# An attention and routed-MLP kernel: another order of the first units, wider matmuls there, and a first batch whose rows are picked by a 0/1 product

## The chip, the cores and the metric

The kernel runs on one core of one Trainium2 chip. The metric is the device time in microseconds, the median of several runs. TensorE (PE) multiplies, VectorE (DVE) and ScalarE (ACT) work elementwise, GpSimd (POOL) does small elementwise work and issues the gathers and scatters, and SyncE (SP) issues nearly all other transfers. Each engine works through its own list in order; semaphores tie the lists together.

## The reference

The inputs q, k, v are 8 batches x 8 heads x 576 positions x 64, in float32. The first part is linear attention; the second routes 128 of the 576 rows of each batch through an MLP:

```python
q_s = softmax(q, axis=-1)                 # over the 64 columns
k_s = softmax(k, axis=2)                  # over the 576 positions
kv = einsum('bhsd,bhse->bhde', k_s, v)    # 64 x 64 for each head
x = einsum('bhsd,bhde->bhse', q_s, kv)    # then heads side by side: (8, 576, 512)

scores = einsum('bsd,d->bs', x, w_gate)
out = x.copy()
for b in range(8):
    top = argpartition(-scores[b], 128)[:128]
    y = maximum(x[b, top] @ w1, 0) @ w2   # 512 -> 1024 -> 512
    out[b, top] = x[b, top] + sigmoid(scores[b, top])[:, None] * y
```

## The kernel before

The work is cut into 16 units: unit u is half of the heads (four) of batch u // 2. The 576 positions of a head lie on 128 partitions in five blocks of 64 or 128 rows, and each step has two halves (`i`), one for each pair of heads.

For one unit the steps are: `load` brings k, v and q; `k_exp`, `q_exp` (ScalarE) take exponentials; `v_copy` puts v beside a column of ones; `kv_mm` multiplies exp(k) by v, 20 matmuls; `kv_out` takes the reciprocal of the sums (`krec`), copies the product to `kv_w` and adds a column, the product with the gate weights `wg`; `q_t` turns exp(q) with TensorE into PSUM, from where one operation for each half scales it by `krec` into `qT`; `x_mm` multiplies `qT` by `kv_w`; `x_out` scales the result by the reciprocals of q's sums into `xs` and writes the sums for the score; `x_store` sends `xs` to the output.

For one batch follow: `score` (adds the gate's sums), `score_row` (five TensorE transposes lay the scores along the free axis on every partition; ScalarE copies them to `srow`), five `compare`, each counting for 128 rows how many scores are larger (`rank`), and `pick`: it compares the rank with the slot numbers to a 0/1 tile `hit`, multiplies this by row numbers and scores on TensorE, and gathers the 128 rows from the output in memory (`xr`). `gate` makes the sigmoid, `turn` transposes the rows to `xT`, eight pieces `mlp1` (four 128x128x128 products each) and eight pieces `mlp2` (one 128x128x512 each) are the MLP, and `finish` adds `xr` to the gated result and scatters it.

The order is written out by hand; nothing is rearranged later. Units 0 to 3 run in a first loop (lines 520 to 566) with `fill`, matmuls on ones whose result nobody reads. Then stage s (lines 571 to 628) runs, for unit s, `q_t`, `x_mm`, `x_out`, `x_store`, for unit s + 1 `kv_mm` and `kv_out`, and between them the MLP of batch (s - 4) // 2: `mlp1` in even stages, `mlp2` in odd ones. A load tile serves every third unit (`LD = 3`). Every transfer takes one of eight semaphores in turn, so that it waits for the transfer eight places before it. PSUM banks rotate by two under each of the names `tp`, `x` and `mm`; a step that writes a bank waits until the bank's last contents are read. At the end a number tells whether all sums are in range; if not, `general` computes everything once more in another way. It isn't entered here.

Of the kernel before, what the change touches and what calls it, by code (L numbers as in the profile page):

```python
# [8 lines left out]
F32 = mybir.dt.float32  # L9
# [8 lines left out]
def kernel(  # L18
# [39 lines left out]
    WARM = 20  # L58
# [4 lines left out]
    n_sl = -(-capacity // P)  # L63
    cuts = [capacity * i // n_sl for i in range(n_sl + 1)]
# [18 lines left out]

    units = [(b, qd) for b in range(B) for qd in range(NQ)]
# [7 lines left out]
    def load(u, which, queue=nc.sync):  # L92
        b, qd = units[u]
        for what in which:
            src = {"q": q, "k": k, "v": v}[what]
            t = raw[what][u % LD]
            first = src[b, 4 * qd].offset
            for n, rows in ((1, N2), (0, R)):
                queue.dma_start(
                    out=t[n::2, :, :rows].rearrange("p h r d -> p h (r d)"),  # L100
                    in_=bass.AP(tensor=src.tensor, offset=first + n * R * D,
                                ap=[[9 * D, 64], [SD, 4], [1, rows * D]]))
# [5 lines left out]
    load(0, "k")  # L108
    load(0, "v", nc.scalar)
    load(0, "q")  # L110
    load(1, "kvq")
    load(2, "kvq")

# [7 lines left out]

    wg = const.tile([P, NQ, 2, D], F32, name="wg")
    for h in range(2):
        nc.scalar.dma_start(out=wg[part(h)].rearrange("p a i d -> p (a i) d"),
                            in_=bass.AP(tensor=moe_w_gate.tensor, offset=moe_w_gate.offset + h * D,
                                        ap=[[0, 64], [2 * D, 2 * NQ], [1, D]]))
    warm = const.tile([P, 1], F32, name="warm")
    nc.scalar.activation(out=warm, in_=ones_b[:, :1], func=AF.Exp)
    w1 = const.tile([P, KD, F], F32, name="w1")
    w2 = const.tile([P, KF, DM], F32, name="w2")  # L130

# [55 lines left out]
    for r in range(R):  # L187
        nc.vector.tensor_scalar(not_before[:, r], order_minus_p, float(r * P), TINY, op0=OP.is_ge, op1=OP.mult)
# [42 lines left out]
    def q_t(u, i):  # L231

        if i == 0:
            st["qT", u] = at.tile([P, 2, R, 2, D], F32, tag="qT", name="qT")
        qe = st["qe", u] if i == 0 else st.pop(("qe", u))
        t_ps = ps.tile([P, 2, 512], F32, tag="x", name="x", bufs=2)
        for r in range(R):
            for a in range(2):
                nc.tensor.transpose(out=t_ps[:, a, r * 64:(r + 1) * 64],  # L239
                                    in_=qe[part(a), i, r].rearrange("p h d -> p (h d)"),  # L240
                                    identity=ident[part(a), part(a)])
        nc.scalar.activation(out=st["qT", u][:, i].rearrange("p r a c -> p a r c"),  # L242
                             in_=t_ps[:, :, :R * 64].rearrange("p a (r c) -> p a r c", r=R),
                             func=AF.Copy, scale=krec[:, u, i:i + 1])

    def x_mm(u, i):
# [4 lines left out]
        for r in range(R):  # L251
            for h, c in QUARTERS:
                nc.tensor.matmul(out=x[part(c), h, r * C:(r + 1) * C], lhsT=qT[part(h), i, r, c],  # L253
                                 rhs=kv_w[u % 2][part(h), i], start=True, stop=True)
# [4 lines left out]
    def x_out(u, i):  # L259
        b, qd = units[u]  # L260
        if qd == 0 and i == 0:
            xs[b] = xp.tile([P, R, NQ, 2, 2, D], F32, tag="xs", name="xs")
            sr[b] = md.tile([P, NQ * 2, G], F32, tag="sr", name="sr")
        x = st.pop(("x", u, i))[:, :, :R * C].rearrange("p h (r c) -> p h r c", r=R)
        rec = qrec[:, u, i].rearrange("p (h r) -> p h r", h=2)
        nc.vector.reciprocal(out=rec, in_=x[:, :, :, D])  # L266
        nc.vector.tensor_mul(xs[b][:, :, qd, i].rearrange("p r h d -> p h r d"), x[:, :, :, :D],  # L267
                             rec.to_broadcast([P, 2, R, D]))
        nc.vector.tensor_mul(sr[b][:, 2 * qd + i].rearrange("p (h r) -> p h r", h=2), x[:, :, :, D + 1], rec)

    def x_store(u):
        b, qd = units[u]
        for n, rows in enumerate((R, N2)):
            nc.sync.dma_start(
                out=bass.AP(tensor=out.tensor, offset=out[b, n * R].offset + 4 * D * qd,
# [4 lines left out]
    def score(b, up=2):  # L280

        raw_s = s_all[:, b]
        nc.vector.reduce_sum(out=raw_s, in_=sr.pop(b).rearrange("p a (h r) -> p r a h", h=2),
                             axis=AX.XY)
        s = md.tile([P, R], F32, tag="s", name="s")
        nc.vector.tensor_mul(s, raw_s, valid_r[:, up])
        nc.vector.tensor_add(s, s, valid_r[:, 1])
# [3 lines left out]
        for c in range(2, NV):  # L291
            nc.gpsimd.tensor_copy(out=vals[:, b, :, c], in_=raw_s if c == 2 else left)
            if c < NV - 1:
                nc.gpsimd.tensor_sub(left, raw_s if c == 2 else left, vals[:, b, :, c])

    def score_row(b):
        s = st["s", b]
        srow = md.tile([P, RP], F32, tag="srow", name="srow")
        for r0, r1 in ((0, N2), (N2, R)):
            t_ps = bank("tp", 2)  # L300
            for r in range(r0, r1):
                nc.tensor.transpose(out=t_ps[:, (r - r0) * P:(r - r0 + 1) * P],
                                    in_=s[:, r:r + 1].to_broadcast([P, P]), identity=ident)
            if r0 == 0:
                nc.scalar.copy(out=srow[:, :N2 * P], in_=t_ps)
            else:
                nc.scalar.copy(out=srow[:, N2 * P:], in_=t_ps[:, :P:2])  # L307
# [21 lines left out]
    def pick(b):  # L329

        rank = st.pop(("rank", b))
        st.pop(("s", b)), st.pop(("srow", b))
        for n, (k0, m) in enumerate(slots):
            hit = md.tile([P, R, P], BF16, tag="hit", name="hit", bufs=1)
            nc.vector.tensor_tensor(out=hit[:, :, :m], in0=slot_no[:, None, k0:k0 + m].to_broadcast([P, R, m]),
                                    in1=rank.to_broadcast([P, R, m]), op=OP.is_equal)
            c_ps = bank("tp", 2)
            for r in range(R):
                nc.tensor.matmul(out=c_ps[:m, :NV], lhsT=hit[:, r, :m], rhs=vals[:, b, r],
                                 start=(r == 0), stop=(r == N2))  # L340
            no = sl.tile([P, 2], F32, tag="no", name="no")
            idx = sl.tile([P, 1], I32, tag="idx", name="idx")
            nc.vector.reduce_sum(out=no[:m, 0:1], in_=c_ps[:m, 0:2], axis=AX.X)
            nc.vector.tensor_scalar(idx[:m], no[:m, 0:1], float((b + 1) * S - 1), None, op0=OP.min)  # L344
            nc.vector.reduce_sum(out=no[:m, 1:2], in_=c_ps[:m, 2:NV], axis=AX.X)  # L345
            xr = sl.tile([P, DM], F32, tag="xr", name="xr")
            nc.gpsimd.indirect_dma_start(  # L347
                out=xr[:m], out_offset=None, in_=out_rows[:(b + 1) * S],
                in_offset=bass.IndirectOffsetOnAxis(ap=idx[:m, :1], axis=0))
            st["pick", b, n] = xr, no, idx  # L350

    def gate(b, n):
        m = slots[n][1]
        xr, no, idx = st["pick", b, n]
        g = sl.tile([P, 1], F32, tag="g", name="g")
# [3 lines left out]
        st["pick", b, n] = xr, g, idx  # L359


    def turn(b, n):
        m = slots[n][1]
        xr = st["pick", b, n][0]
        xT = sl.tile([P, KD, P], F32, tag="xT", name="xT")
        t_ps = bank("mm", 2)
        for d in range(KD):
            nc.tensor.transpose(out=t_ps[:, d * m:(d + 1) * m], in_=xr[:m, d * P:(d + 1) * P],  # L368
                                identity=ident[:m, :m])
        nc.scalar.copy(out=xT[:, :, :m], in_=t_ps[:, :KD * m].rearrange("p (d c) -> p d c", d=KD))  # L370
# [23 lines left out]

    def finish(b, n):
        m = slots[n][1]
        xr, g, idx = st.pop(("pick", b, n))
        y_ps = st.pop(("y", b, n))
        o = sl.tile([P, DM], F32, tag="o", name="o")
        nc.vector.scalar_tensor_tensor(o[:m], y_ps[:m], g[:m], xr[:m], op0=OP.mult, op1=OP.add)  # L400
        nc.gpsimd.indirect_dma_start(  # L401
            out=out_rows[:(b + 1) * S], out_offset=bass.IndirectOffsetOnAxis(ap=idx[:m, :1], axis=0),
            in_=o[:m], in_offset=None)
# [34 lines left out]
    def general():  # L438
        for b in range(B):
# [16 lines left out]
            score_row(b)  # L456
            for r in range(R):
                compare_exact(b, r)
            pick(b)
            each(gate, b)  # L460
# [9 lines left out]
    def sums_in_range():  # L470
# [5 lines left out]
        for n, (src, op, bound) in enumerate(((rq, OP.max, 1.0 / LOW), (rk, OP.max, 1.0 / LOW), (sc, OP.max, FAR),  # L476
# [3 lines left out]
                                    op0=OP.is_le if op == OP.max else OP.is_ge)  # L480
        g_ps = bank("tp", 2)
# [8 lines left out]
    LAG = 4  # L490

    def load_w1(n):
        nc.sync.dma_start(out=w1[:, n], in_=moe_w1[n * P:(n + 1) * P])

    def load_w2(n):
        half = KF // 2
        nc.sync.dma_start(out=w2[:, n * half:(n + 1) * half],
                          in_=moe_w2[n * half * P:(n + 1) * half * P].rearrange("(f p) d -> p f d", p=P))

    EARLY = 4  # L500

    def fill(n):

        junk_ps = bank("mm", 2)
        for _ in range(n):
            nc.tensor.matmul(out=junk_ps, lhsT=ones_b[:, :P], rhs=ones_b, start=True, stop=True)

# [6 lines left out]
    k_exp(0)  # L514
    v_copy(0)
    kv_and_exp(0)
    load(3, "kvq")


    for s in range(EARLY):  # L520
        q_t(s, 0)
        q_t(s, 1)
        k_exp(s + 1)
        v_copy(s + 1, nc.gpsimd)
        fill(2)
        x_mm(s, 0)
        x_mm(s, 1)
        fill(2)
        if s == 2:
            kv_mm(s + 1)  # L530
            q_exp(s + 1, 0)
            fill(3)
            pick(0)
            x_out(s, 0)
            kv_out(s + 1)
            x_out(s, 1)
            x_store(s)
            q_exp(s + 1, 1)
        else:
            x_out(s, 0)  # L540
            x_out(s, 1)
            x_store(s)
# [114 lines left out]
```

## Time and profile before

| | us |
|---|---|
| median of three runs | 218.88 (217.52 to 220.17) |
| the profiled execution | 217.89 |
| its span, first to last instruction | 216.0 |
| TensorE busy | 197.5 |
| VectorE busy | 116.2 |
| ScalarE busy | 88.6 |
| GpSimd busy | 34.4 |
| transfers | 46.81 MB, 217 GB/s over the span |

Row 1 of the page gives busy time of each engine, its share of the span and the number of its instructions. The slices cut the span into 40 pieces of 5.4 us; a digit is the busy share in tenths. A line of the timeline or of a group reads: start, length, engine, line of the kernel, operation, what is written and what is read, number; in brackets the idle time of the engine ahead of it and what ended it. `PE` is the matmul itself, `PEld` the load of its weights. A float32 matmul is two records. Matmuls overlap, so that their price is the difference of two starts. A line of a table of windows has the stretch, its length, busy time and number for PE, PEld, DVE, ACT and POOL, then TensorE's clock, the share of the DMA engines and GB/s. In the chain of work that ended last, a line has a start, a length, the engine and what it did.

### The profile page before, as it was taken

Reading aid. Unit: us, or ns where it says so; the run is one execution under the profiler, and the core shown is the slowest. Engines: PE = TensorE matmul, PEld = TensorE weight load, DVE = VectorE, ACT = ScalarE, POOL = GpSimd, SP = SyncE. Lnnn points to the kernel's source line nnn. Section 1 sums busy time; section 2 is a strip of 40 time slices with the busy share of each in tenths; the row PEclk is TensorE's granted clock in tenths of the full one; section 3 lists DMA queues with packets and bytes.
Section 4 is the critical chain, followed back from the end, with each engine's and each line's share of the span. In section 5 each row is a group of like instructions: output and inputs, shape, how many; then the busy total and the mean of one; then the engine's idle time right before and its main releaser. Section 6 shows DMA issues by size and latency. Waiting matters only on the chain. (4 is left out here: it accounts for less than half of the span.)

```text
span 216.0 us, 7090 instructions
## 1 busy us (share of the span) xinstructions
PE 197.5 (91%) x3040; PEld 147.2 (68%) x3040; DVE 116.2 (54%) x359; ACT 88.6 (41%) x146; POOL 34.4 (16%) x78
## 2 busy tenths in 40 slices
PE   5987595999999999999999999999999989999960
PEld 2464462799749975897679776996599548749620
DVE  6552595668726774477626872596358665501010
ACT  2386374763626471746265443536263311211100
POOL 6022402300112012200320023001120112101010
PEclk9999999999999999999999999999999999999996
DMA  5999999999999997958594949421313041101001
GB/s 179 299 356 358 375 398 369 362 392 377 377 384 381 375 344 249 314 157 283 171 320 154 313 133 303 161 82 49 113 52 109 7 156 52 49 3 52 5 5 52
DMA packets 39335, 46.81 MB, mean 217 GB/s; under 512 B 2944, under 2 KB 36736, under 8 KB 39296
## 3 DMA queue, kind: packets, MB, share of 16 engines
q1 hardware_dynamic: 36928, 41.36, 56.4%
q0 software_dynamic: 1280, 4.20, 5.7%
q10 hardware_dynamic: 1088, 0.72, 1.1%
q8 instruction: 26, 0.43, 0.8%
q14 instruction: 13, 0.11, 0.2%
HBM read 34.73 MB, written 11.53 MB: 214 GB/s over the span
## 5 line engine op out<-in xcount | busy, mean ns | idle before, releaser
L382 PE MATMUL mm<-xT,w 128*128 128x128 f32 x512 | 62.1, 278 | 0.0
L382 PEld LDWEIGHTS mm<-xT,w 128*128 128x128 f32 x512 | 58.8, 192 | 2.3 <-ACT xT L370 1.5
L392 PE MATMUL mm<-w,hT 128*128 128x512 f32 x128 | 59.9, 603 | 0.0
L315 DVE SCALAR_TENSOR_TENSOR junk<-srow,s,not_before 128x576 bf16<-128x576 f32 x40 | 32.8, 819 | 8.3 <-ACT srow L307 7.2
L392 PEld LDWEIGHTS mm<-w,hT 128*128 128x128 f32 x128 | 22.5, 190 | 21.2 <-issue 20.4
L267 DVE TENSOR_TENSOR xs<-x,qrec 128x640 f32<-128x640 f32 x32 | 26.4, 825 | 1.1
L242 ACT ACTIVATE qT<-x,krec 128x640 f32<-128x640 f32 x32 | 23.9, 792 | 6.2 <-PE x L239 6.1
L400 DVE SCALAR_TENSOR_TENSOR o<-mm,g,xr 128x512 f32<-128x512 f32 x8 | 6.0, 751 | 37.7 <-PE mm L392 37.7
L202 ACT ACTIVATE qe<-q 128x640 f32<-128x640 f32 x32 | 23.6, 739 | 3.0 <-DMA q<-in_q_dram 2.8
L215 PE MATMUL tp<-v_ones,ke 128*64 128x65 f32 x640 | 22.6, 224 | 2.3 <-issue 2.1
L215 PEld LDWEIGHTS tp<-v_ones,ke 128*64 128x64 f32 x640 | 20.3, 137 | 5.3 <-issue 3.0
L253 PE MATMUL x<-kv_w,qT 64*64 64x66 f32 x1280 | 22.4, 221 | 0.0
L347 POOL DMA_INDIRECT xr<-out_dram,idx x8 | 8.0, 996 | 88.8 <-DVE qrec L266 72.6
L253 PEld LDWEIGHTS x<-kv_w,qT 64*64 64x64 f32 x1280 | 20.2, 134 | 2.6 <-ACT qT L242 0.8
L195 ACT ACTIVATE ke<-k 128x1280 f32<-128x1280 f32 x16 | 20.3, 1270 | 2.8 <-DMA k<-in_k_dram 2.8
L385 ACT ACTIVATE hT<-mm 128x512 f32<-128x512 f32 x16 | 9.5, 596 | 28.7 <-PE mm L382 28.7
L239 PEld LDWEIGHTS x<-ident,qe 64*128 64x128 f32 x320 | 11.7, 139 | 11.6 <-issue 5.0
L239 PE MATMUL x<-ident,qe 64*128 64x64 f32 x320 | 14.5, 229 | 4.9 <-issue 1.4
L266 DVE RECIPROCAL qrec<-x 128x10 f32<-128x10 f32 x32 | 6.9, 215 | 20.7 <-PE x L253 20.7
L401 POOL DMA_INDIRECT out_dram<-o,idx x8 | 10.1, 1269 | 46.8 <-DVE o L400 46.8
L226 ACT COPY kv_w<-tp 128x130 f32<-128x130 f32 x16 | 4.3, 266 | 31.4 <-DVE krec L224 31.4
L370 ACT COPY xT<-mm 128x512 f32<-128x512 f32 x8 | 4.7, 585 | 26.9 <-PE mm L368 26.9
(81 smaller groups left out, 126.0 us busy)
## 6 DMA issues: line engine op xcount, KB each, us to landing
k<-in_k_dram SPq DMA_DIRECT2D x16, 320.0 KB, 7.0
q<-in_q_dram SPq DMA_DIRECT2D x16, 320.0 KB, 6.1
out_dram<-xs SPq DMA_DIRECT2D x16, 320.0 KB, 2.9
v<-in_v_dram SPq DMA_DIRECT2D x15, 320.0 KB, 7.9
k<-in_k_dram SPq DMA_DIRECT2D x16, 256.0 KB, 7.2
q<-in_q_dram SPq DMA_DIRECT2D x16, 256.0 KB, 6.4
out_dram<-xs SPq DMA_DIRECT2D x16, 256.0 KB, 3.2
v<-in_v_dram SPq DMA_DIRECT2D x15, 256.0 KB, 7.7
```

Source lines behind the costliest of these rows:

```text
L195: nc.scalar.activation(out=ke, in_=raw["k"][u % LD], func=AF.Exp)
L202: nc.scalar.activation(out=st["qe", u][:, i], in_=qr[:, i], func=AF.Exp)
L215: nc.tensor.matmul(out=kv[part(h), i], lhsT=ke[:, 2 * i + h, r], rhs=vo[:, 2 * i + h, r], start=(r == 0), stop=(r == N2))
L239: nc.tensor.transpose(out=t_ps[:, a, r * 64:(r + 1) * 64], in_=qe[part(a), i, r].rearrange("p h d -> p (h d)"), identity=ident[part(a), pa ...
L242: nc.scalar.activation(out=st["qT", u][:, i].rearrange("p r a c -> p a r c"), in_=t_ps[:, :, :R * 64].rearrange("p a (r c) -> p a r c", r= ...
L253: nc.tensor.matmul(out=x[part(c), h, r * C:(r + 1) * C], lhsT=qT[part(h), i, r, c], rhs=kv_w[u % 2][part(h), i], start=True, stop=True)
L267: nc.vector.tensor_mul(xs[b][:, :, qd, i].rearrange("p r h d -> p h r d"), x[:, :, :, :D], rec.to_broadcast([P, 2, R, D]))
L315: nc.vector.scalar_tensor_tensor(junk, st["srow", b], st["s", b][:, r:r + 1], not_before[:, r], op0=OP.subtract, op1=OP.is_ge, accum_out=s ...
L382: nc.tensor.matmul(out=h_ps[:, f % 4 * m:(f % 4 + 1) * m], lhsT=w1[:, d, f * P:(f + 1) * P], rhs=xT[:, d, :m], start=(d == 0), stop=(d == ...
L385: nc.scalar.activation(out=hT[:, f - 3:f + 1, :m], in_=h_ps[:, :4 * m].rearrange("p (f c) -> p f c", f=4), func=AF.Relu)
L392: nc.tensor.matmul(out=st["y", b, n][:m], lhsT=st["hT", b, n][:, f, :m], rhs=w2[:, f], start=(f == 0), stop=(f == KF - 1))
L401: nc.gpsimd.indirect_dma_start(out=out_rows[:(b + 1) * S], out_offset=bass.IndirectOffsetOnAxis(ap=idx[:m, :1], axis=0), in_=o[:m], in_off ...
```

## The change

- The batches are worked in another order: batch `b` of the program is batch `(b - 1) % 8` of the data (`place`), so that the first one stands last in the output.
- Units 0 to 2 use a wide form: `q_t` has five 128x128 transposes for each half, not ten of 64 partitions; `x_mm` has ten matmuls with 128 columns of weights, not twenty of 64x64. For two halves VectorE scales `qT` in ScalarE's place. The fills are gone, and `WARM` falls from 20 to 12.
- The gate weights come as one row of 512, and two matmuls with ones spread them over the partitions. Three of five masks `not_before` are made later.
- `x_out` is parted into `x_sums` (the score's sums) and `x_scale`, so that the score can be taken before the scaling. `score_row` reads the raw scores, and ScalarE multiplies by the constant while it copies. GpSimd makes the masked scores `s`.
- For batch 0, `select` multiplies the rows in `xs` by a 0/1 tile on TensorE after each `compare`, which gives `xT` without memory. Its stores come in stage 5, its gather in stage 16, its last addition (`finish_rows`, on GpSimd) and scatter in stage 17.
- The stages begin with unit 3 (`LAG = 3`). In stages 3, 5 and 7 (`OWN`) the unit's own `kv_mm` runs in the stage, and that of the next unit at its end.
- Loads: k of unit 0 on two queues, then v and q, units 1 and 2, all of w1 in two column halves, unit 3, half of w2, unit 4, the other half; then unit s + 2 in stages 3 to 5, unit 8 in stage 6, 9 and 10 in stage 7, 11 and 12 in stage 8.

```diff
-    WARM = 20
+    WARM = 12
+    def place(b):
+        return (b - 1) % B
...
-    def q_t(u, i):
+    def q_t(u, i, on_vector=False, wide=False):
...
+        if wide:
+            to = st["qT", u][:, i].rearrange("p r a c -> p (r a c)")
+            src = t_ps.rearrange("p a c -> p (a c)")[:, :R * P]
+            for r in range(R):
+                nc.tensor.transpose(out=src[:, r * P:(r + 1) * P], in_=qe[:, i, r].rearrange("p h d -> p (h d)"),
+                                    identity=ident)
...
+        if on_vector:
+            nc.vector.tensor_scalar(to, src, krec[:, u, i:i + 1], None, op0=OP.mult)
...
+    def select(b, n, r):
+        k0, m = slots[n]
+        if r == 0:
+            st["select", n] = bank("mm", 2), md.tile([P, R, P], F32, tag="hit_f", name="hit_f", bufs=1)
+        t_ps, hit = st["select", n]
+        nc.vector.tensor_tensor(out=hit[:, r, :m], in0=slot_no[:, k0:k0 + m],
+                                in1=st["rank", b][:, r:r + 1].to_broadcast([P, m]), op=OP.is_equal)
+        row = xs[b][:, r].rearrange("p a i h d -> p (a i h d)")
+        for d in range(KD):
+            nc.tensor.matmul(out=t_ps[:, d * m:(d + 1) * m], lhsT=row[:, d * P:(d + 1) * P], rhs=hit[:, r, :m],
+                             start=(r == 0 and d == 0), stop=(r == N2 and d == KD - 1), skip_group_check=True)
+        if r == N2:
+            turned(b, n, t_ps)
...
+    def finish_gated(b, n):
+        m = slots[n][1]
+        o = sl.tile([P, DM], F32, tag="o_gated", name="o_gated", bufs=n_sl)
+        nc.scalar.activation(out=o[:m], in_=st.pop(("y", b, n))[:m], func=AF.Copy, scale=st.pop(("g", b, n))[:m])
+        st["o", b, n] = o
+    def finish_rows(b, n):
+        m = slots[n][1]
+        o = st.pop(("o", b, n))
+        nc.gpsimd.tensor_add(o[:m], o[:m], st.pop(("xr", b, n))[:m])
+        put(b, n, o)
...
+    ready(0)
+    q_exp(0, 0)
+    kv_mm(0)
...
+    set_not_before(range(2))
+    nc.vector.tensor_copy(out=wg.rearrange("p a i d -> p (a i d)"), in_=g_ps[:, :4 * D])
+    kv_out(0)
+    q_exp(0, 1)
...
+    q_t(0, 0, wide=True)
+    q_t(0, 1, on_vector=True, wide=True)
+    set_not_before(range(2, R))
+    ready(1, nc.gpsimd)
+    x_mm(0, 0, wide=True)
+    x_mm(0, 1, wide=True)
+    x_out(0, 0)
+    x_out(0, 1)
+    kv_mm(1)
...
+    x_sums(1, 0)
+    x_sums(1, 1)
+    score(0)
+    kv_mm(2)
+    score_row(0, tag="mm")
+    kv_out(2)
+    x_scale(1, 0)
+    x_scale(1, 1)
+    q_t(2, 0, wide=True)
+    q_t(2, 1, wide=True)
+    k_exp(3)
+    for r in range(R):
+        compare(0, r)
+        if r == N2 - 1:
+            x_mm(2, 0, wide=True)
+        for n in range(n_sl):
+            select(0, n, r)
...
+    LAG = 3
+    OWN = 3, 5, 7
+    for s in range(LAG, NU + LAG):
...
+        own = s in OWN
+        kv_next = s + 1 < NU and not own and s + 1 not in OWN
...
+        if own:
+            if s > LAG:
+                ready(s)
+            pieces(2)
+            kv_and_exp(s)
...
+        if here:
+            q_t(s, 0)
+            q_t(s, 1)
+        if chosen is not None:
+            each(hits, chosen)
+        if kv_next:
+            ready(s + 1)
+        if own:
+            pieces(1)
+        else:
+            pieces(2)
+        if chosen is not None:
+            each(find, chosen)
+            each(fetch, chosen)
+        if here:
+            x_mm(s, 0)
+            x_mm(s, 1)
+            x_sums(s, 0)
+            x_sums(s, 1)
+            if ends is not None:
+                score(ends)
+            x_scale(s, 0)
+            x_scale(s, 1)
+            x_store(s)
+        if s == 5:
+            x_store(0)
+            x_store(1)
+        if kv_next:
+            kv_and_exp(s + 1)
...
+        pieces(1)
+        if own:
+            v_copy(s + 1)
+        if ends is not None:
+            score_row(ends)
+            if own:
+                k_exp(s + 1)
+            for r in range(R):
+                compare(ends, r)
+        if s == LAG:
+            each(hits, 0)
+            each(find, 0)
...
+        pieces(1 if own else 3)
+        if own:
+            kv_and_exp(s + 1)
+        pieces(1)
+        if second and mlp_b + 1 < B:
+            each(turn, mlp_b + 1)
+        pieces(KF - f_next)
+        if second:
+            each(finish if mlp_b else finish_gated, mlp_b)
+        if s == NU + 1:
+            each(finish_rows, 0)
```

In the changed order `hits` is the 0/1 tile of `pick`, `find` its product with row numbers and scores, `fetch` its gather; `ready` is `k_exp` and `v_copy`, and `turned` the copy to `xT`.

## The prediction

> **What bounds the kernel now.** I read the page's busy row and slices first, then the chain that ended last, then TensorE's timeline by stage.
>
> ```profile
> PE 197.5 (91%) x3040; PEld 147.2 (68%) x3040; DVE 116.2 (54%) x359; ACT 88.6 (41%) x146; POOL 34.4 (16%) x78
> PE   5987595999999999999999999999999989999960
> DMA  5999999999999997958594949421313041101001
> ```
> TensorE is full from about 40 us on and has holes before; the DMA engines are full until about 80 us. The chain's pieces at the end:
>
> ```profile
> 187.12 6.21 PE mm L392 x14
> ...
> 194.62 7.28 PE mm L382 x64
> 201.91 6.88 PE mm L392 x16
> ...
> 208.81 0.76 DVE o L400
> ...
> 210.12 0.69 POOL out_dram L401
> ```
> So the end is TensorE's last matmul (208.8) plus a tail of 7.2 us. One even stage of the full stretch:
>
> ```profile
> 87.37 0.84 PE L239 MATMUL x<-ident,qe 64*128 64x64 f32 x20
> 88.14 2.05 PE L382 MATMUL mm<-xT,w 128*128 128x128 f32 x16
> 90.12 1.40 PE L253 MATMUL x<-kv_w,qT 64*64 64x66 f32 x80
> 91.45 1.39 PE L215 MATMUL tp<-v_ones,ke 128*64 128x65 f32 x40
> 92.77 1.16 PE L382 MATMUL mm<-xT,w 128*128 128x128 f32 x8
> 93.76 0.71 PE L302 MATMUL tp<-ident,s 128*128 128x128 f32 x5
> 94.31 4.63 PE L382 MATMUL mm<-xT,w 128*128 128x128 f32 x40
> 98.87 0.84 PE L239 MATMUL x<-ident,qe 64*128 64x64 f32 x20
> ```
> Differences of starts are prices: q_t 0.77, x_mm 1.33, kv_mm 1.32, score_row 0.55, eight mlp1 pieces 7.53. The odd stage gives mlp2 7.18, find 0.20, turn 0.43. From 42.64 (first mlp1) to 208.8 this is 164.25 of work and 1.9 of holes. Where the start goes, and one wait:
>
> ```profile
> 19.42 0.40 PE L239 MATMUL x<-ident,qe 64*128 64x64 f32 x6 [1.35 <-issue]
> 27.39 0.82 DVE L315 SCALAR_TENSOR_TENSOR junk<-srow,s,not_before 128x576 bf16<-128x576 f32 x1 [0.34 <-ACT srow L307]
> 33.97 1.17 POOL L347 DMA_INDIRECT xr<-out_dram,idx  x1 [7.55 <-DVE qrec L266]
> 42.64 2.05 PE L382 MATMUL mm<-xT,w 128*128 128x128 f32 x16
> 173.62 0.76 PE L302 MATMUL tp<-ident,s 128*128 128x128 f32 x5 [1.36 <-DVE s L287]
> ```
> Batch 0's ranking starts at 27.39, but its rows come back from memory only for the mlp1 at 42.64. At 173.62 TensorE waits 1.36 for a score with eight ready mlp2 matmuls behind.
>
> **The Trainium skill.** "TensorE: Matmul & The Clock Gate", Part 1: the clock halves after about 3.4 us without work and opens after as much busy time. The trace agrees; work ended at 208.8:
>
> ```profile
> 209.00:211.00 2.00, 0.00 (x0) 0.00 (x0) 0.56 (x1) 0.00 (x0) 0.97 (x1) 1.00 0.01 4
> 212.00:213.00 1.00, 0.00 (x0) 0.00 (x0) 0.00 (x0) 0.00 (x0) 0.00 (x0) 0.60 0.10 37
> 213.00:214.00 1.00, 0.00 (x0) 0.00 (x0) 0.00 (x0) 0.00 (x0) 0.00 (x0) 0.50 0.00 0
> ```
> The third number from the right is the clock. The same page, Part 2: matmuls keep program order, as at 173.62. "Runtime: NRT & Kernel Launch", Instruction fetch mechanics: instructions come in 16 KiB blocks of 256; here 26 fetches moved 0.43 MB, and "issue" holes of 1.35 (19.42) and 2.09 (25.56) lie 254 instructions apart.
>
> **The start.** I walk through each engine's list in the changed order, at the trace's durations and 0.15 to 0.2 a handover (kv_mm follows ke by 0.17 at 9.22). Times in us:
> - Unit 0's k goes out on two queues, the 128 KB of broadcast gate weights shrink to one row, and the five masks (0.38 each) no longer precede v_copy: I take v landed at 7.0 (now 7.5), v_copy 0.82, kv_mm(0) 8.05 (now 9.22) to 9.4.
> - The gate row's two matmuls (new, 0.4 to 0.9) end at 10.0; wg's copy, reciprocal, kv_w 0.27 and q_exp 0.74 make 11.75; q_t to 12.45; the scaled copy on VectorE (new; 0.83 as its nearest row, the xs product from PSUM; 0.4 to 0.9) to 13.4; three masks to 14.6; two x_out of 1.25 to 17.1. So unit 1's reciprocal is at 17.15, now 16.57: the early lead is used up on VectorE.
> - kv_w, q_exp: 18.35; q_t and scaled copy: 20.0; x_mm to 20.8; sums, score: 21.65.
> - kv_mm(2) from 20.8, score_row to 22.7; srow, then kv_w(2) on ScalarE to 23.9; product and its sum to 24.55; two scalings 1.7: the ranking starts at 26.25, now 27.39.
> - Five pairs of compare (0.87) and 0/1 tile (new, 128 columns: 0.2 to 0.4 with its wait), 5.75: 32.0. The last select (four matmuls of two 0.113 passes), xT 0.58, handovers: mlp1 at **33.5**, 9.1 earlier. Bounds 31 (short new operations) and 36 (fetch holes stay).
>
> The wide forms: a 128-column transpose is 0.11 (score_row), so q_t costs 1.1, not 0.77; x_mm I take as before (0.6 to 1.2 a half). The two gate-row matmuls, 0.4 to 0.9. They lie where TensorE waits anyway. The 27 fills (about 5.9 busy) sat in holes: nothing, unless the clock drops. Fewer early instructions put the first block edge (about the 440th) in kv_mm(2), its block having landed: both fetch holes gone (0 to 2). DMA: w1's first half has 6.4 MB ahead of or in it, k of unit 3 8.0 MB; at the measured 0.36 MB/us, with some 1 MB in flight, they land at 23 and 28, before need. ke(3) stands ahead of xT on ScalarE, so k after 31.5 would delay 33.5.
>
> **Work after the start.** Stage 3 now has q_t, x_mm, two kv_mm, score_row, find and mlp1: 13.0. Stages 4 to 8: 9.9, 12.8, 9.9, 12.8, 11.2. Stages 9 to 18 keep the old prices. Sum 170.25, +6.0: two q_t, one x_mm, two kv_mm and a find have moved behind the first mlp1.
>
> **New holes on TensorE.** (a) Stage 3: find(0) stands ahead of four mlp1 pieces and kv_mm(4), and waits for hits(0), last in VectorE's list. After x_mm(3) VectorE has sums and score 0.9, two scalings 1.7, v_copy 0.83, five compares 4.35, hits 0.83: 8.6. TensorE has one piece and score_row, 1.5. Hole **7.2**. Nothing hides it: gate(0) needs find only later. (b) In stages 3, 5, 7 kv_mm(s) runs in its own stage, so q_t's second half waits for reciprocal, kv_w and q_exp, 1.15 each: 3.45. (c) Stage 3's kv_mm waits for v_copy: 0.25. (d) Stages 5 and 7 open with mlp1, not q_t, and its bank frees only when ScalarE or VectorE has read y: 0.95 and 0.75, 1.7 together. (e) kv_mm(6), kv_mm(8) wait for k_exp behind hT and srow on ScalarE: 1.45 each; then the reciprocal is behind five compares: 0.45 each: 3.8. Sum 16.4; before 1.9, whose 1.36 the earlier score removes. (f) After 7.2 idle the clock is low: 1.7, half of 3.4.
>
> From stage 9 on I find no hole: after x_mm VectorE needs 9.0 up to hits, TensorE has 10.0 ahead of find. What moves costs nothing there: batch 0's two stores (1.2 MB, 3.2 us of transfer) stand ahead of unit 7's loads on SP's queue, which land about 5 us before use; gate(0) has stage 4; its fetch stands ahead of batch 7's on POOL (0.97; rows needed 4.4 after, median landing 3.9: 0 to 1); the late addition is some 1.1 by an estimate from "GPSIMD Engine Reference", 3.1 (4497 ns at 2048; no run here shows it), 15 us before the last put.
>
> Sum: -9.1 + 6.0 + 14.5 + 1.7 = **+13.1**. Span 216.0 to 229.1; with the 1.9 around it (217.89 - 216.0) 231.0 for a profiled execution. The median shown, 218.88, is 1.0 above that execution: **232**.
>
> **Rivals.** *No holes (faster).* VectorE is ahead of TensorE in stages 3 to 8 and the holes close to about 1.2: -9.1 + 6.0 - 0.7 = -3.8, **215**. For it: a full TensorE for 170 us now; against it: the orders above leave TensorE nothing to run. It decides where holes and cold clock stay under 2.8 in sum. *Cold start.* 12 warm-up matmuls end at 7.4, just where their pace now goes from 0.43 to 0.2, and no fill follows. If the clock stays low, some 5 us of matmuls on the path double: **237**. For it: holes of 1 to 3 us up to 33; against: now holes of 2 left it open. *Little change.* Half the holes fill and mlp1 starts by 30.5: 232 - 9 - 3 = **220**.
>
> **How the numbers follow.** Forecast 0.70 (222 to 235), cold start 0.15, little change 0.06, no holes 0.09. Bounds of the start -2.5 to +2.5, of the holes about 4 either way: 222 to 239 leaves out the two lower rivals and a tail. Faster by over 1% 0.09, within 0.06, slower 0.85; one per cent is about what this kernel's spread of runs can tell.
>
> **What would show it.** The first L457 matmul (mlp1) near 33.5; find(0) (L389) on TensorE with some 7 us idle ahead, released by the 0/1 tile; 1 us holes ahead of q_t in stages 3, 5, 7; clock under 1.0 after find; later batches still 22.7. Wrong if find(0) waits under 2 us or mlp1 starts before 30.

## The result, and the profile after

The changed kernel takes 234.0 us (median of 4 executions, 233.5 to 234.87), the kernel before beside it 219.52 (217.52 to 220.29): 1.068 times as long, with a 95% interval of 1.060 to 1.076. The forecast was 232. The profiled execution took 233.84, its span is 232.0 in place of 216.0. A second set of the changed kernel gave 1.0696 (e0 below). Ratios and their intervals, here and below, leave out executions that took over 1.5% longer than the fastest one of their kernel.

From the page of the changed kernel: the busy row, and the slices (5.8 us each) of TensorE, of its clock and of the transfers.

```profile
PE 204.8 (88%) x2895; PEld 157.5 (68%) x2895; DVE 119.6 (52%) x353; ACT 87.1 (38%) x145; POOL 36.7 (16%) x93
PE   6688598719998899988999999999999999999980
PEclk9999799985999999999999999999999999999996
DMA  5999999083058199915999996958413041321101
```

TensorE has 145 matmul records fewer and yet is busy 7 us longer. The slice with a 1 in its row (46.4 to 52.2 us) and the 8 and 5 of the clock in and behind it are the place that the forecast named. The transfers now have gaps from 40 us on, where before they were full until about 80.

The start, from the timeline of TensorE, with VectorE's last 0/1 tile among it, and from the windows of the same stretch (the clock is the third number from the right):

```profile
27.37 4.12 PE L418 MATMUL mm<-hit_f,xs 128*128 128x128 f32 x24
31.25 0.29 DVE L414 TENSOR_TENSOR hit_f<-slot_no,rank 128x128 f32<-128x128 f32 x1
31.42 1.33 PE L286 MATMUL x<-kv_w,qT 64*128 64x66 f32 x20
32.68 2.05 PE L418 MATMUL mm<-hit_f,xs 128*128 128x128 f32 x16
34.67 1.33 PE L286 MATMUL x<-kv_w,qT 64*128 64x66 f32 x20
35.93 2.05 PE L457 MATMUL mm<-xT,w 128*128 128x128 f32 x16
```

```profile
25.00:28.00 3.00, 2.36 (x13) 2.02 (x14) 2.97 (x7) 1.18 (x2) 0.00 (x0) 0.75 1.06 358
28.00:30.00 2.00, 2.00 (x12) 2.00 (x12) 1.93 (x7) 1.56 (x2) 0.00 (x0) 0.53 1.05 380
```

VectorE's last tile is done at 31.54, where the forecast had 32.0. But TensorE is behind it: its clock was 0.50 from 26.5 to 29.5, it has worked off only three `select` by 31.42, then `x_mm(2, 0)` stands ahead of the other two, and `x_mm(2, 1)` ahead of `mlp1`. The first `mlp1` is at 35.93, not 33.5; before it was at 42.64.

The hole of stage 3, from the timeline and the windows:

```profile
50.58 0.82 DVE L379 TENSOR_TENSOR hit<-slot_no,rank 128x640 bf16<-128x640 f32 x1
51.46 0.29 PE L389 MATMUL tp<-vals,hit 128*128 128x5 bf16 x5 [6.29 <-DVE hit L379]
51.61 2.05 PE L457 MATMUL mm<-xT,w 128*128 128x128 f32 x8
53.59 2.44 PE L235 MATMUL tp<-v_ones,ke 128*64 128x65 f32 x40
55.96 3.53 PE L457 MATMUL mm<-xT,w 128*128 128x128 f32 x24
```

```profile
52.00:53.00 1.00, 1.00 (x6) 1.00 (x6) 0.20 (x2) 0.00 (x0) 0.00 (x0) 0.50 0.98 312
```

`find(0)` waits 6.29 for the 0/1 tile. VectorE works from 43.60 to 51.40 without a hole, in the order that the forecast gave: its list behind `x_mm(3)` takes 7.9, forecast 8.6. Behind `find(0)` a piece of `mlp1` costs 1.98 and `kv_mm(4)` 2.37, at the full clock 0.99 to 1.07 and 1.31.

The smaller waits, from the timeline, and from the chain that ended last a piece that recurs in stages 9, 11 and 13:

```profile
40.58 0.53 PE L270 MATMUL x<-ident,qe 64*128 64x64 f32 x10 [0.76 <-ACT qe L222]
80.42 1.39 PE L235 MATMUL tp<-v_ones,ke 128*64 128x65 f32 x40 [1.01 <-ACT ke L215]
```

```profile
148.85 1.37 PE x L291 x80
150.93 1.46 DVE xs L313 x2
153.47 4.47 PE mm L457 x40
```

VectorE's scalings stand in the chain: `kv_out`'s product comes behind them and frees its PSUM bank late, so that the fifth transpose of `score_row` waits for it (`DVE prod`, three times, 0.9 together; some 0.33 a batch with the handover). A batch takes 23.06 (first `mlp1` 146.80 to 169.86) in place of 22.7.

The account of the 16 us, in one table, for this one profile. The holes, (a) to (e), are idle times with their handover: the difference of two starts, less the undisturbed price.

| term | forecast | measured |
|---|---|---|
| first `mlp1` earlier | -9.1 | -6.7 |
| work moved behind it | +6.0 | 6.0, and about 1.6 for the finer cuts |
| (a) `find(0)` | 7.2 | 6.4 |
| (b) second half of `q_t`, stages 3, 5, 7 | 3.45 | 2.9 |
| (c) `v_copy` in stage 3 | 0.25 | 0.1 |
| (d) y's bank, stages 5, 7 | 1.7 | 0.1 |
| (e) `kv_mm(6)`, `kv_mm(8)`, `q_t` behind | 3.8 | 2.5 |
| (f) clock behind `find(0)` | 1.7 | 2.6 |
| later gathers, holes without a releaser, `score_row`, the last count | 0 to 1 | about 0.8, 0.6, 1.0, 0.4 |
| the old holes | -1.9 | -1.9 |
| tail | 0 | -0.3 |
| sum, span | +13.1 | +16.0 (terms: 16.1) |

The finer cuts: without any hole a stage with its own `kv_mm` takes 13.3 (from the `mlp1` at 58.76 to the `q_t` at 72.08 in e9 below), not the 12.8 of the forecast, since `mlp1` is cut into five groups there, and a group of one piece costs 0.98 to 1.09 in place of 0.94 (7.53 for eight); 0.5 in each of three stages.

### The profile page after: what moved, and what is told of

Its sections match the earlier page's. It is cut to its first block, busy times and chain, and to the rows that moved or that the text cites. A ratio compares the mean times of both kernels' runs of the same rounds, so it can differ in the third digit from the quotient of the medians.

```text
span 232.0 us, 6810 instructions
## 1 busy us (share of the span) xinstructions
PE 204.8 (88%) x2895; PEld 157.5 (68%) x2895; DVE 119.6 (52%) x353; ACT 87.1 (38%) x145; POOL 36.7 (16%) x93
## 4 chain that ended last, share of the span: by engine, by line
PE 73%; DVE 11%; DMA 6%; ACT 5%; issue 2%; POOL 0%; POOLq 0%; ACTq 0%; DVEq 0%
PE mm L457 23%; PE mm L467 21%; PE tp L235 8%; PE x L291 7%; PE x L270 4%; DMA xr<-out_dram,idx 4%; DVE xs L313 3%; PE mm L418 3%; DMA v<-in_v_dram 2%; PE x L286 2%; DVE junk L362 2%; ACT ke L215 2%; PE mm L438 2%; PE x L263 1%; ACT qe L222 1%
## 5 line engine op out<-in xcount | busy, mean ns | idle before, releaser
L457 PE MATMUL mm<-xT,w 128*128 128x128 f32 x512 | 65.7, 283 | 0.0
L457 PEld LDWEIGHTS mm<-xT,w 128*128 128x128 f32 x512 | 60.9, 196 | 3.7 <-ACT xT L445 1.9
L235 PE MATMUL tp<-v_ones,ke 128*64 128x65 f32 x640 | 23.7, 230 | 3.9 <-ACT ke L215 2.0
L313 DVE TENSOR_TENSOR xs<-x,qrec 128x640 f32<-128x640 f32 x32 | 24.9, 815 | 0.0
L276 ACT ACTIVATE qT<-x,krec 128x640 f32<-128x640 f32 x30 | 22.5, 791 | 5.9 <-PE x L270 3.2
L291 PE MATMUL x<-kv_w,qT 64*64 64x66 f32 x1040 | 18.7, 221 | 0.2 <-issue 0.2
L445 ACT COPY xT<-mm 128x512 f32<-128x512 f32 x8 | 4.7, 585 | 34.7 <-PE mm L438 29.5
L291 PEld LDWEIGHTS x<-kv_w,qT 64*64 64x64 f32 x1040 | 16.7, 134 | 1.3 <-issue 0.4
L472 POOL DMA_INDIRECT out_dram<-o,idx x7 | 8.3, 1182 | 53.1 <-DVE o L480 53.1
L270 PEld LDWEIGHTS x<-ident,qe 64*128 64x128 f32 x260 | 9.5, 139 | 6.8 <-ACT xT L445 3.0
L270 PE MATMUL x<-ident,qe 64*128 64x64 f32 x260 | 11.8, 229 | 2.3 <-ACT qe L222 2.3
```

The source lines that it names most:

```text
L235: nc.tensor.matmul(out=kv[part(h), i], lhsT=ke[:, 2 * i + h, r], rhs=vo[:, 2 * i + h, r], start=(r == 0), stop=(r == N2))
L270: nc.tensor.transpose(out=t_ps[:, a, r * 64:(r + 1) * 64], in_=qe[part(a), i, r].rearrange("p h d -> p (h d)"), identity=ident[part(a), pa ...
L276: nc.scalar.activation(out=to, in_=src, func=AF.Copy, scale=krec[:, u, i:i + 1])
L457: nc.tensor.matmul(out=h_ps[:, f % 4 * m:(f % 4 + 1) * m], lhsT=w1[:, d, f * P:(f + 1) * P], rhs=xT[:, d, :m], start=(d == 0), stop=(d == ...
```

## The experiments

Ratios are to the kernel before on the same chip. e1 to e4 ran on a chip where the kernel before took 223.64 us (223.02 to 227.03), and the changed kernel wasn't run there. A late batch takes 23.6 in the profiles of e1, e2 and e3, in place of 23.05 in those of e0 and e5; why was not tried. So these four are read by the first 65 us of their profiles, and their ratios beside the 1.068 are only a rough guide. e0 and e5 to e7 ran together, e8 to e10 together, e11 alone.

**e0, the changed kernel again.** No edit.

> The changed kernel as it stands, beside the others of this set and the kernel before, so that differences to it can be taken on one chip. Expected: 1.068 times the kernel before, first L457 matmul at 35.9 us, find(0) at 51.5 with 6.3 idle ahead of it.

234.16 us, ratio 1.0696 (1.0639 to 1.0754). `find(0)` at 50.07 with 6.29 idle. But the first `mlp1` came at 34.55: here the clock was full from 24 to 33 us. So the start's half clock belongs to some executions, not to all. Nor was the early start worth anything in this one: its span is 232.0 too, and the `mlp1` of stage 9 begins at 123.68, in the first profile at 123.75. The lead went into waits for transfers in stage 8, where the first profile shows none. From e0's timeline:

```profile
114.82 1.39 PE L235 MATMUL tp<-v_ones,ke 128*64 128x65 f32 x40 [0.59 <-DVE no L393]
121.46 0.66 PE L438 MATMUL mm<-ident,xr 128*128 128x128 f32 x4 [0.77 <-DMA xr<-out_dram,idx]
```

The first names VectorE, which had itself waited 2.81 for unit 9's v.

**e1, `find(0)` later.**

```diff
+        if s == LAG + 1:
+            each(hits, 0)          # after fetch(chosen), stage 4
...
+        if s == LAG + 1:
+            pieces(1)
+            each(find, 0)
+            each(gate, 0)          # after x_store
...
-        if s == LAG:
-            each(hits, 0)
-            each(find, 0)
```

`gate(0)` came at the start of stage 4 and moves along; the piece of `mlp2` ahead of `find(0)` is taken from the three behind it.

> The changed kernel, but the 0/1 tile and the find of batch 0 move from stage 3 to stage 4, behind batch 1's find; nothing is left out. Theory (the find in stage 3 stops TensorE 6.5 us for VectorE's list, and costs 2.7 more because the clock is half after it): both go, and a wait of some 1.8 us appears ahead of the second half of q_t(4), whose reciprocal is behind the five compares; the median falls by about 7.4 us, to 226 to 228. Rival (TensorE is late there for transfers, and the find only shows it): the hole moves to kv_mm(4) or to the first mlp2 and the median stays within 2 us of 234.

228.77 us, ratio 1.0209 (1.0104 to 1.0313). Stage 5 starts at 61.47 (69.24 in the changed kernel; 0.43 of that is the earlier first `mlp1`): 7.3 less. The hole is gone, the clock is 1.00 from 50 to 56, and one wait has come in its place: not the 1.8 expected ahead of `q_t(4)`, but one ahead of `kv_mm(4)`. From e1's timeline:

```profile
46.63 1.39 PE L235 MATMUL tp<-v_ones,ke 128*64 128x65 f32 x40 [1.01 <-ACT ke L215]
```

So (a) and (f), 9.0 together in the changed kernel, came from one position in the list. 7.3 of it is net gain: this wait, which the long one had covered, takes 1.07 with its handover, and `x_mm(4)` and `q_t(4)` take 0.4 and 0.2 longer (1.73 and 0.98). The median, 228.77, lies above the 226 to 228 expected, on a chip where the kernel before is slower too.

**e2, matmuls in the hole.** 28 matmuls whose result nobody reads, ahead of `hits(0)`.

```diff
         if s == LAG:
+            fill(28)
             each(hits, 0)
             each(find, 0)
```

> The changed kernel with 28 matmuls on ones, whose result nobody reads, in the hole ahead of find(0) in stage 3 (about 4.5 us at full clock); the find stays where it is. Theory: the hole stays as long, the clock stays at 1.00 behind it, and f4, kv_mm(4) and f5 to f7 take their usual 5.1 us and not 7.8; the median falls by 2.7 us. Rival (what follows the find is slow for another reason, the instruction fetch or transfers): these take 7.8 us as before and the median stays at 234.

235.03 us, ratio 1.0493 (1.0384 to 1.0601). `find(0)` still comes only at 50.38, 15.53 behind the first `mlp1` as in the changed kernel (35.93 to 51.46), for its 0/1 tile is no earlier. But what follows runs at the full clock. From e2's timeline:

```profile
50.38 0.28 PE L393 MATMUL tp<-vals,hit 128*128 128x5 bf16 x5 [0.84 <-DVE hit L383]
51.59 1.39 PE L235 MATMUL tp<-v_ones,ke 128*64 128x65 f32 x40
52.90 2.94 PE L461 MATMUL mm<-xT,w 128*128 128x128 f32 x24
```

From `find(0)`'s successor to `q_t(4)` it takes 5.26 (50.52 to 55.78), in the changed kernel some 7.8. (f) is thus 2.6, and it is the clock: 1.00 from 50 to 56 here, 0.50 from 51 to 57 in the changed kernel. It is apart from (a).

**e3, matmuls in the start.** Nine that nobody reads, ahead of `kv_out(2)`.

```diff
     score_row(0, tag="mm")
+    fill(9)
     kv_out(2)
```

> The changed kernel with 9 matmuls on ones behind the score row of batch 0, where TensorE idles from 23.3 to 25.6 us. Theory (the clock fell to half at about 26.8, and this made the select products pile up on TensorE, so that the last ended 3.1 us after the last 0/1 tile): the clock stays at 1.00 and the first mlp1 starts at about 33.5 and not 35.9; the median falls by 2.4 us. Rival (the wide x_mm and the number of select products fill TensorE even at full clock): the first mlp1 stays within 0.7 us of 35.9.

237.05 us, ratio 1.0567 (1.0426 to 1.0707). The clock is 1.00 from 25 to 30, the first `mlp1` at 34.66: 1.3 less than in the first profile of the changed kernel (0.4 of it from an earlier `kv_mm(0)`), but 1.2 above the 33.5 that the theory gave, and no earlier than e0, whose clock was full without it. Neither theory held: half clock is worth about 0.9, and something else more. With e7, below, it can be read.

**e4, the narrow forms** in units 0 to 2.

```diff
-    q_t(0, 0, wide=True)
+    q_t(0, 0)
...
-        if r == N2 - 1:
-            x_mm(2, 0, wide=True)
+        if r == N2 - 1:
+            x_mm(2, 0)
```

> The changed kernel with the old narrow q_t and x_mm for units 0 to 2 too; all else as changed. Theory: x_mm is 0.67 a half and not 1.2, q_t 0.4 and not 0.7, so that TensorE reaches the last select about 1 us sooner: first mlp1 at 34.5 to 35.5, the median 0.5 to 1.5 us lower. Rival (the wide form is what keeps the instruction fetch from stopping TensorE): holes of 1 to 2 us named issue come back by 25 us, and the first mlp1 is later than 36.

236.59 us, ratio 1.0548 (1.0427 to 1.0669). First `mlp1` at 35.73, later than the 34.5 to 35.5 expected. The rival's holes didn't come either: one named `issue` is there, 0.18. A half of `x_mm(2)` takes 0.75 in place of 1.26, but the clock was 0.57 from 18 to 22 us and 0.50 from 30 to 32, so that three selects took 4.58. Gain and loss cancel; whether the narrow form is better here stays open.

**e5, both halves of `q_exp` ahead of `kv_out`** in stages 3, 5, 7.

```diff
             pieces(2)
-            kv_and_exp(s)
+            kv_mm(s)
+            q_exp(s, 0)
+            q_exp(s, 1)
+            kv_out(s)
```

> In stages 3, 5 and 7 both halves of q_exp are issued ahead of kv_out, so that q_t's second half has its operand when it is reached. Theory (those waits, 0.96 each in the profiled execution, stand on TensorE's path): 2.9 us less than the changed kernel. Rival (what TensorE gains is lost at the next handover, since kv_w and the scaled copies come later by one q_exp, 0.74, and x_mm waits for them): 0 to 1 us less.

231.39 us, ratio 1.0565 (1.0505 to 1.0625), 2.8 less than e0 on the same chip. The wait is gone: `q_t(3)` is one group of 20, and 0.76 later comes `mlp1`.

```profile
38.25 0.83 PE L270 MATMUL x<-ident,qe 64*128 64x64 f32 x20
```

(b) is confirmed, at 0.96 a stage, and within the noise all of it was on the path.

**e6, four edits of the order together:** e1, e5, and

```diff
         if here:
             q_t(s, 0)
             q_t(s, 1)
+        if own:
+            k_exp(s + 1)           # was behind score_row
...
                 score(ends)
+                if kv_next:
+                    kv_and_exp(s + 1)   # was behind x_scale, from stage 9 on
             x_scale(s, 0)
```

> Four edits of the order together: find(0) and gate(0) at the end of stage 4; both halves of q_exp ahead of kv_out in stages 3, 5, 7; k_exp(s + 1) there right after q_t, ahead of hT and srow on ScalarE; from stage 9 on kv_out ahead of x_scale on VectorE. Theory (the loss is the sum of holes on TensorE, and they are independent): find 7.3, q_t 2.9, kv_mm 3 x 1.05 = 3.1, score_row 3 x 0.33 = 1.0, together 14.3 less than the changed kernel, that is level with the kernel before (ratio 0.99 to 1.01). Rival (the other engines can't keep up in stages 3 to 8, and holes come back elsewhere there): at most 9 less, ratio 1.02 or above.

223.71 us; ratio 1.0163 (1.0097 to 1.0229), from the four executions of 220.8 to 224.0. Two others took 227.5 and 228.0, and the profiled one is of these. Its windows:

```profile
9.00:15.00 6.00, 5.67 (x56) 4.06 (x51) 1.45 (x6) 3.04 (x5) 1.25 (x1) 0.50 1.07 367
15.00:22.00 7.00, 7.00 (x81) 6.76 (x82) 4.37 (x11) 1.06 (x2) 1.25 (x1) 0.50 1.06 375
```

That fits the forecast's cold start: the 12 warm-ups ended at 6.69, TensorE stood 2.09 for `kv_mm(0)`, and then ran at half clock for 13 us; the first `mlp1` came at 40.05. By the ratios the four edits give 11.7 us (1.0696 less 1.0163, of 218.78), where 14.3 were expected and the rival had at most 9: between the two. What is missing lies in waits that came up in place of the ones removed: 0.56 to 0.57 ahead of `kv_mm(4)`, `(6)` and `(8)`, 0.39 to 0.45 ahead of the second half of `q_t` in stages 4, 6 and 8 (as in the profiles of e7 and e8), 2.9 together. Of the four edits only the first two were also run alone (e1, e5).

**e7, e6 and an earlier queue:** the nine matmuls of e3, and `x_mm(2, 0)` after the second comparison.

```diff
-        if r == N2 - 1:
+        if r == 1:
             x_mm(2, 0, wide=True)
```

> The four edits, and in the start nine matmuls whose results nobody reads ahead of kv_out(2), and x_mm(2, 0) after the second comparison in place of the fourth, so that TensorE has less queued when the last 0/1 tile comes. Theory (half clock and queue on TensorE made the start's last 2.4 us): first mlp1 at 33.5 to 34, another 1.5 to 2.4 less than with the four edits alone, so 0.985 to 0.995 of the kernel before. Rival (VectorE's comparisons end later, for x_mm(2, 0) doesn't matter there): within 0.7 of the four edits alone.

222.13 us, ratio 1.0147 (1.0103 to 1.0191): by the ratios 0.35 below e6, within the rival's 0.7, though the executions lie closer (221.7 to 222.9). The rival's reason doesn't hold: VectorE's last tile starts 22.62 behind `kv_mm(0)`, in the changed kernel 22.63. The first `mlp1` is at 34.45, again not 33.5. But with the clock at 1.00 throughout, e7's timeline shows what the start's end is made of:

```profile
27.07 1.16 PE L422 MATMUL mm<-hit_f,xs 128*128 128x128 f32 x8 [0.23 <-DVE hit_f L418]
28.15 1.33 PE L286 MATMUL x<-kv_w,qT 64*128 64x66 f32 x20
29.42 3.84 PE L422 MATMUL mm<-hit_f,xs 128*128 128x128 f32 x32
33.19 1.33 PE L286 MATMUL x<-kv_w,qT 64*128 64x66 f32 x20
```

From the first select on TensorE has no hole: five selects take 1.08 + 3.77, two halves of `x_mm(2)` 1.27 + 1.26, together 7.38. VectorE needs 1.07 for a comparison and its tile, 5.3 for five. So TensorE is the limit there, by 2 us, even at the full clock.

**e8, e6 with 16 warm-ups** (`WARM = 16`).

> The four edits of the order, and 16 warm-up matmuls in place of 12; nothing else. With the four edits alone two of six executions took 227.5 to 228, the other four 220.8 to 224; in the profiled one of the two the clock was 0.50 from 15 to 22 us and the first mlp1 came at 40.0 in place of 34.5. Theory (the cold start of the forecast's rival: after 12 warm-ups TensorE idles up to 2.1 us ahead of kv_mm(0), and then computes too little to open the clock): with 16 the hole ahead of kv_mm(0) is under 1 us, the clock is full from 10 us on, no execution is above 225, median 221 to 222. Rival (the long executions have another cause, such as the loads): they stay as frequent.

223.10 us, ratio 1.0191 (1.0149 to 1.0233), 221.97 to 224.22: no long execution, the wait ahead of `kv_mm(0)` 0.52, the clock 1.00 to 22 us. The median is 1 above the expectation, 221 to 222: the 2.32 wait ahead of `q_t(2)` is still there, and behind it the clock was 0.76 from 27 to 32. None of the 34 executions with 16 warm-ups (e8, e9, e11) is above 224.8. Two of six against none isn't much of a count, since 10 executions of the changed kernel itself, with 12 warm-ups, show no such one either (one of e3's four took 241.3 where the others took 236.5 to 237.4, and has no profile). e6's windows show what happens in one such execution, not how often it comes, and that the warm-ups are its cure is not shown.

**e9, all of it:** e7, 16 warm-ups, `v_copy` on GpSimd in stages 3, 5, 7, both halves of `q_exp` ahead of `kv_out` at their ends too, and `x_mm(2, 1)` ahead of the last select.

```diff
         if own:
-            k_exp(s + 1)
+            ready(s + 1, nc.gpsimd)
...
-        if own:
-            v_copy(s + 1)
...
         if own:
-            kv_and_exp(s + 1)
+            kv_mm(s + 1)
+            q_exp(s + 1, 0)
+            q_exp(s + 1, 1)
+            kv_out(s + 1)
```

> The four edits, the early fill, 16 warm-ups, and for the holes that were left (0.57 and 2 x 0.56 ahead of kv_mm(4), (6), (8) for v_copy; 0.45, 0.39, 0.40 ahead of the second half of q_t in stages 4, 6, 8): v_copy on GpSimd in stages 3, 5, 7, both halves of q_exp ahead of kv_out at their ends, and x_mm(2, 1) ahead of the last select, where it costs about 0.4 less. Theory: 2.9 + 0.4 less than with four edits and fill, thus 218.5 to 219.5, level with the kernel before (ratio 0.996 to 1.006). Below it there is little to find: the first mlp1 is 8 us earlier, but 6 us of attention work now lie behind it. Rival (holes behind a faster TensorE turn into waits for transfers and instruction fetches): less than half of it, 221 or more.

222.35 us, ratio 1.0136 (1.0091 to 1.0182): the rival was right. The waits for `v_copy` and `q_exp` are gone (stage 5 starts at 58.76), and TensorE then waits for transfers. From e9's timeline:

```profile
103.02 1.39 PE L235 MATMUL tp<-v_ones,ke 128*64 128x65 f32 x40 [2.00 <-DVE no L397]
110.03 0.66 PE L442 MATMUL mm<-ident,xr 128*128 128x128 f32 x4 [1.14 <-DMA xr<-out_dram,idx]
```

As in e0, the first line names VectorE, which itself had waited 3.34 for unit 9's v. And the first `mlp1` came 0.68 late (35.51): with `x_mm(2, 1)` ahead of the last select nothing covers the copy of `xT`.

**e10, the kernel before with the early score alone,** for the last unit (`x_sums` and `x_scale` as in the change).

```diff
+        if last:
+            x_sums(s, 0)
+            x_sums(s, 1)
+            score(ends)
+            x_scale(s, 0)
+            x_scale(s, 1)
+            x_store(s)
+        elif here:
...
-        if last:
-            score(ends)
```

> The kernel before with one part of the change alone: for the last unit the sums and the score are made ahead of the two scalings. Theory (forecast: the earlier score removes the 1.36 us wait of score_row at 173.62, which stands on TensorE's path): 1.0 to 1.4 less than the kernel before, ratio 0.994. Rival (the ranking behind it still waits for both scalings on VectorE, and the last batch's rows set the end): no difference, ratio 0.998 to 1.002.

217.86 us (15 executions), the kernel before 219.18; ratio 0.9945 (0.9920 to 0.9970), 1.2 us less. From its timeline, the line that answers to 173.62 of before:

```profile
173.05 0.76 PE L319 MATMUL tp<-ident,s 128*128 128x128 f32 x5 [0.23 <-DVE s L304]
```

1.36 has become 0.23. The forecast's step is confirmed, and this part of the change is a gain by itself.

**e11, e9 with `x_mm(2, 1)` back behind the last select, and earlier loads.**

```diff
+        if s == LAG:
+            load(5, "kvq")
...
-        if s < 6:
-            load(s + 2, "kvq")
-        elif s == 7:
-            load(9, "kvq")
-            load(10, "kvq")
+        if s < 8:
+            load(s + 3, "kvq")
```

> As the kernel with all edits (222.35), but x_mm(2, 1) is again behind the last select, and units 5 to 10 are loaded earlier: unit 5 at the start of stage 3, then unit s + 3 in stages 3 to 7. There kv_mm(9) stood 2.00 us for unit 9's v at 103.02, the gathers ahead of 110.03 and 81.60 came 1.14 and 0.29 late, and the first mlp1 stood 0.68 for the copy of xT, which x_mm(2, 1) covers if it comes behind. Theory (what the edits gained was given back to transfers that start too late): 3.0 to 4.1 less, thus 218.3 to 219.4, level with the kernel before. Rival (the DMA engines are short of rate there, whatever the order; other transfers are late in turn): within 1.5 of the kernel with all edits.

218.43 us (22 executions), the kernel before 219.72; ratio 0.9934 (0.9901 to 0.9967). By the ratios that is 4.4 less than e9, so the theory held, and a little more. The waits for transfers are gone; of stages 3 to 18 three holes are left, one ahead of the last count (0.38) and two without a releaser:

```profile
75.65 0.46 PE L291 MATMUL x<-kv_w,qT 64*64 64x66 f32 x11 [0.18 <-issue]
89.23 0.68 PE L291 MATMUL x<-kv_w,qT 64*64 64x66 f32 x27 [1.33 <-issue]
```

The first `mlp1` is at 34.60, the last matmul ends at 209.48. Over all 22 and 27 executions the means are 218.78 and 219.69, a ratio of 0.996. So e11 and e10 both come out below both kernels, by about half a per cent; they weren't run on one chip, and which is faster stays open.

## Why the prediction was right

The direction, the size and the main mechanism held: 234.0 measured, 232 forecast, and the holes on TensorE carry it. That the sum came within 3 us of span (+13.1 against +16.0) is in part luck, for errors of both signs meet in it: holes and clock, (a) to (f), were 18.1 in the forecast and 14.6 on the chip, while the start came 2.4 later than forecast, and the finer cuts (1.6) and the later waits (2.8) weren't in the sum. Point by point:

- *The first mlp1, 33.5: 2.4 too early, the term most mis-sized.* The walk-through was right on VectorE (ranking from 26.14, forecast 26.25; last tile 31.54, forecast 32.0). The step that failed is "Five pairs of compare and 0/1 tile ... The last select": it prices the ranking on VectorE and of TensorE's part only the last select. All five selects at the price named there (four matmuls of two 0.113 passes, 0.9 each) and two halves of `x_mm` make 7 us on TensorE, against 5.75 on VectorE; e7 measured 7.38. Half clock added about 0.9 to the start in some executions (from `kv_mm(0)` to the first `mlp1` 27.3 with it, 26.4 in e0 without); e0's time was no shorter for it. The wide `x_mm`, 1.26 a half, came out just above its upper bound of 1.2.
- *Hole (a), 7.2: 6.4, and (f), 1.7: 2.6.* e1 took both away by one move, e2 parted them. (a) was smaller since VectorE's list took 7.9, not 8.6: the sums of the first half run beside `x_mm`'s second. (f) was larger since the low clock lasted from 51 to 57 us, not for the 3.4 us that the forecast took. Together they were 8.9 in the forecast and 9.0 on the chip.
- *(b) and (e): right in place, 0.96 and 1.08 each instead of 1.15 and 1.45.* e5 took (b) away. In e6 some 0.56 was left of each wait ahead of `kv_mm`, and 0.4 ahead of `q_t`; in e9, with `v_copy` on GpSimd and both `q_exp` first, neither shows.
- *(d), 1.7: wrong.* The two pieces at 69.24 take 2.10, those at 95.90 1.96, against 1.98 undisturbed. No wait for y's bank shows: at 69.24 `mlp1` starts before ScalarE begins to read y (69.44). The kernel before, where the last `mlp1` follows `mlp2` directly (at 194.62), had none either. Why the bank doesn't hold `mlp1` up was not tried.
- *"From stage 9 on I find no hole": wrong by 0.33 a batch.* The move of the sums ahead of the scaling has a price that the forecast didn't look for: `kv_out` stands behind both scalings, and with it the bank of `score_row`. e7, where `kv_out` goes first, has 22.72 a batch again (136.36 to 159.08).
- *"Both fetch holes gone": right for the start.* Later `x_mm(6)` took 1.92 in place of 1.33, around an idle time of 0.23 named `issue`; that this is an instruction fetch is not shown.
- *The late addition, 1.1 by the forecast's estimate: 1.28* on GpSimd, from 212.39, some 14 us before the last put (226.20).
- *The early score removes 1.36: right* (e10).
- *The rivals.* The cold start exists: e6's profile has it in full, and one more execution of e6 was as long. The profile of the changed kernel doesn't have it; there the clock fell later, behind another wait (0.53 in 28 to 30). No holes, 215, needed a TensorE without waits: e11 comes near that state, at 0.9934 of the kernel before, about 217.4 for its 218.88. There the first `mlp1` leads by 8.0, 6 us of moved work and 1.6 of finer cuts take it back; what is left is small, as the forecast's own sum for that rival said (-3.8 with a lead of 9.1).

## What to carry to other kernels

A step that is brought forward pays only up to what it leaves behind it: here 6 us of attention work and a list of steps that had been covered came to stand behind the first `mlp1`. Walk each new stage through on every engine, the one that receives the new operations first, and sum its whole queue there, not only the last item. Waits that are taken out bring up others that they had covered: here first those of other engines, then those of the transfers, so that the loads had to move with the rest.

## What was not expected of the hardware

- Between executions of the same instructions the clock of the start differed: 0.58 from 26 to 29 us in one profile of the changed kernel, 1.00 in another (e0), behind the same wait of 2.32 us ahead of `q_t(2)`. "TensorE: Matmul & The Clock Gate", Part 1, in the Trainium skill says that the window of about 3.4 us runs freely and that the clock's turn depends on its phase. That one wait lowered the clock in some executions only fits this. But its table of states has the clock fall after at least one idle window, and this wait was shorter than one; the measurement decides. A forecast from one profile can't tell which it will be.
- In e6's profile the clock stayed at 0.50 from 9 to beyond 22 us, while TensorE was busy 5.67 of 6.00 and 7.00 of 7.00 us. The same section has it open after at least one busy window, some 3.4 us. Here it took about four times as long. Why was not tried.
